# Dynamic convolution and two expert layers on one core: the fold of layer one's tail channels moved off TensorE, and loads and float32 groups replanned

## The chip, the cores and the metric

One core of one Trainium2 chip. The metric is the device time of one execution in microseconds (us), lower is better. The kernel before takes 1397.72 us (median of 3 runs, 1397.65 to 1398.44).

## The reference, cut to what matters

```
attn: w = softmax(weight_gen over K=7 taps); x1[s, d] = sum_k w[s, head(d), k] * x[s - 6 + k, d]
layer 1: h = x1 @ w_in;  g = (a0 + a1 h + a2 h^2 + a3 h^3) / (1 + |b0||h| + |b1| h^2 + 1e-6);  x2 = g @ w_out
layer 2: h = x2 @ w_in2; g = h * clip(h + 3, 0, 6) / 6;                       out = g @ w_out2
```

There are 8192 tokens of 192 channels (2 sequences of 4096), 8 heads, and 2048 hidden channels in both layers. The four weight matrices arrive as 64-bit floats; x and weight_gen are float32.

## The kernel before, in words

**Tiling.** The tokens are cut into 32 units of 256, and a block is one unit. Two units share a chunk: one load of x (`load_chunk`, L105) and one softmax (`softmax_a`, `softmax_e`, `softmax_b`, L132 to L156). A layer's 2048 hidden channels are 16 groups of 128; four groups make a slot of 128x1024 values, so a block has 4 slots and the kernel 128.

**One block.** `conv_mul` and `conv_sum` make the convolution, `xT` transposes it on TensorE into PSUM (L206, L207), `x_hi` and `x_lo` split it into a high and a low float32r part. `in1` multiplies with w_in (five float32r matmuls for each group, `mm_in`, L281) into `h1`, of which there are two buffers in PSUM. A long chain over ScalarE, GpSimd and VectorE (`act_u` to `pool_lo`) makes `ghi` and `glo`, and its step `dve_d` (L370) is the last reader of `h1`. `out1` (L397 to L401) multiplies with w_out and sums a block into one PSUM bank `y1` of two halves: the first 128 output channels, and the tail.

**The fold.** The tail has 64 channels. Its weights `wo1s` hold the high parts in columns 0 to 63 and the low parts in columns 64 to 127, so the tail half of `y1` holds two partial sums, on partitions 0 to 63 and 64 to 127, which must be added. Before, `mid_y` (L229) copies the half to the SBUF tile `ys`, `mid_f` (L250) multiplies it in plain float32 with the constant matrix `fold`, which adds the halves and puts the sum on both, into a bank `yf` of the three-bank ring "s"; `mid_tail` (L257) and `tail_lo` (L264) split `yf` into high and low parts. `mid_head` (L236) and `head_lo` (L243) do so for the first half. `in2` (L281 again), `act_r2`, `dve_g2` and `out2` (L438, plain float32) are layer two; `evac` writes the result.

**Weights.** 28 jobs load 64-bit pieces into a staging ring `st` of 4 buffers (L456), ScalarE and VectorE join the two words to a float32 (`low` L490, `scale` L484, `join` L496, `sign` L503), and `hi` and `lo` split it (L510, L511, L533). The SBUF of the staging ring is reused by layer two's tiles, so `mid_y` of block 0 waits until all jobs are done.

**The order of the work** is not written out: `plan()` places every step on PE, ACT, DVE, POOL or SP by an assumed cost, a priority (a due time from the constants T, CH, XQ, UM ...) and the buffers it takes. Each engine then runs its list in order.

Of the kernel before, what the change touches and what calls it, by code (L numbers as in the profile page):

```python
# [8 lines left out]
F32 = mybir.dt.float32  # L9
# [3 lines left out]
AF = mybir.ActivationFunctionType  # L13
ALU = mybir.AluOpType
# [5 lines left out]
def kernel(  # L20
# [63 lines left out]
        late.append(stage.enter_context(tc.tile_pool(name="late", bufs=2)))  # L84

    ident = const.tile([P, P], F32, name="ident")
    fold = const.tile([P, 2, 64], F32, name="fold")
    acol = const.tile([P, 4], F32, name="acol")
    bcol = const.tile([P, 2], F32, name="bcol")
    bab = const.tile([P, 2], F32, name="bab")  # L90
# [11 lines left out]
    wgt = {}  # L102
    wk = {}

    def load_chunk(c):  # L105
        g = two.tile([P, CT * H, K], F32, tag="wg", name="wg")
        nc.sync.dma_start(
            out=g.rearrange("p (t h) k -> p t (h k)", h=H), in_=wgf[:, c * CT : (c + 1) * CT, :]
        )
        t = two.tile([P, ROWS, D], F32, tag="x", name="x")  # L110
        first = c * CT - (K - 1)
        neg = max(0, -first)
        segs = [(0, P)]
        if neg:
            segs = [(b * S // R + 1, (b + 1) * S // R) for b in range(B)]
            for b in range(B):
                p = b * S // R
                nc.gpsimd.memset(t[p : p + 1, 0:neg, :], 0.0)
                nc.sync.dma_start(
                    out=t[p : p + 1, neg:, :], in_=xf[None, b * S : b * S + ROWS - neg, :]  # L120
                )
        for p0, p1 in segs:
            src = bass.AP(
                tensor=xf.tensor,
                offset=xf.offset + (first + p0 * R) * D,
                ap=[[R * D, p1 - p0], [1, ROWS * D]],
            )
            nc.sync.dma_start(out=t[p0:p1].rearrange("p r d -> p (r d)"), in_=src)
        xch[c] = t
        wgt[c] = g  # L130

    def softmax_a(c):  # L132
        g = wgt[c]
# [92 lines left out]

    def mid_y(b):
        ysb[b] = late[0].tile([P, BMAX], F32, tag="ys", name="ys", bufs=1)[:, : BT[b]]
        nc.scalar.activation(out=ysb[b], in_=y1[b][:, BT[b] :], func=AF.Copy)  # L229

    def mid_head(u):
        b, v = UB[u]
# [13 lines left out]
        )  # L246

    def mid_f(b):
        ps = fold_ps[b] = bank(("mid_f", b), [P, 512], "yf")[:, : BT[b]]
        nc.tensor.matmul(  # L250
            out=ps, lhsT=fold.rearrange("p a d -> p (a d)"), rhs=ysb.pop(b),
            start=True, stop=True,
        )

    def mid_tail(u):
        b, v = UB[u]
# [190 lines left out]
        nc.sync.dma_start(out=of[:, u * 2 : u * 2 + 2, :], in_=o)  # L447

    CW = 512
    ST = 4  # L450

    def load_rows(dst, src):
        srcs = src if isinstance(src, list) else [src]
# [127 lines left out]
                    l(eng)  # L581

    G2 = 11
    T = 9.094
    CH = 5.027
    KP = 0.221
    XP = 17
    LP = 43.011
    LOADP = {(0, "load"): -100.0, (1, "load"): -80.0}
    WIN = 29  # L590
    PEN = 1.976
    CP = 3
    JP0 = 0.189
    JPT = 1.514
    HOLD = 6
    URG = 4.005
    UR = 17.898
    UG = 15.269
    SM = 1.345
    CV = 3.0  # L600
    XTP = 2.0
    XQ = 7.596
    I2 = 2.702
    SPR = 0.483
    O2 = 3.176
    OS = 3.771
    O1 = 1.491
    UM = 1.45
    ops = {}

    def op(key, eng, cost, prio, emit, after=(), take=(), lat=0.15):
# [16 lines left out]
    for n, key in enumerate(order):  # L628
        p = JP0 + n * JPT - (30.0 if n < 2 else 0.0)
        f64, split = WS == 2, key[0] != "o2"  # L630
        sz = 1.0 if key[0] in ("in", "pair") else 0.75
        last = ("job", key, "lo" if split else "sign" if f64 else "load")
        wf = [("wf", 3, [last])] if split else []

        def step(k, eng, cost, prev, take=(), lat=0.15, also=[]):
            op(
                ("job", key, k), eng, cost, LOADP.get((n, k), p - LP * (k == "load")), lambda e=None, key=key, k=k: job_step(key, k, e),
                ([("job", key, prev)] if prev else []) + also, take, lat,
            )

        flex = (("POOL", 1.25 * sz, 0.0), ("DVE", 0.62 * sz, PEN))
        step("load", "SP", 1.46 * sz, None, [("st", ST, [("job", key, "sign")])] if f64 else wf, 2.2)
        if f64:
            step("low", "ACT", 0.55 * sz, "load")
            step("scale", "ACT", 0.55 * sz, "load", [("s", NSB, [("job", key, "sign")])])
            step("join", "DVE", 0.61 * sz, "scale", also=[("job", key, "low")])
            step("sign", "DVE", 0.61 * sz, "join", wf)
        if split:
            step("hi", "ACT", 1.6 if key[0] == "pair" else 0.52 * sz, "sign" if f64 else "load")
            step("lo", flex, 0, "hi")  # L650
        done[key] = last
# [2 lines left out]
    TU = [S0[b] * T - (4 * (BV[b] - 1 - v) + XTP) * T for b, v in UB]  # L654
    for c in range(NCH):
        t = TU[2 * c] - CV * T + 1.9
        add("load", "SP", 3.1, t - XQ * T if c else -90.0, load_chunk, c, lat=2.2, take=[
            ("x", 2, [("conv_mul", 2 * c + 1, 1)]), ("wg", 2, [("softmax_b", c)]),
        ])
        add("softmax_a", "DVE", 0.75, t - SM * T + 2.85, softmax_a, c, after=[("load", c)])  # L660
        add("softmax_e", "ACT", 0.28, t - SM * T + 4.1, softmax_e, c, after=[("softmax_a", c)])
        add("softmax_b", "DVE", 1.5, t - SM * T + T + 6.6, softmax_b, c, after=[("softmax_e", c)],
            take=[("wk", 2, [("conv_mul", 2 * c + 1, 1)])])
    for u, (b, v) in enumerate(UB):
        t = TU[u]
        for i in range(2):
            flex = (("POOL", 2.6, 0.0), ("DVE", 1.6, CP))
            add("conv_mul", flex, 0, t + (2 * i - CV) * T + 1.9, conv_mul, u, i,
                after=[("load", u // 2), ("softmax_b", u // 2)],
                take=[("prod", 1, [("conv_sum", u, i, 1)])])  # L670
# [11 lines left out]
    for b in range(len(BL)):  # L682
        sl = S0[b] + NF // BF[b] - 1
        t = (sl + 2) * T
        add("mid_y", "ACT", 0.2 + BT[b] / 1280, t + 6.05 - UM, mid_y, b,
            after=[("out1", sl, 1), ("late",)], take=[("ys", 1, [("mid_f", b)])])
        add("mid_f", "PE", BT[b] / 590, t + 8.2 - UM, mid_f, b, after=[("mid_y", b)],
            take=[("s", NSB, [("tail_lo", B0[b] + BV[b] - 1)])])
        for v in range(BV[b]):
            u = B0[b] + v  # L690
            add("mid_head", "ACT", 0.4, t + 6.1 + v * 0.1 - UM, mid_head, u, after=[("mid_y", b)],
                take=[("xh1", 2, [("in2", u, NP - 1)])])
            add("head_lo", "DVE", 0.42, t + 7.0 + v * 0.5 - UM, head_lo, u,
                after=[("mid_head", u)] + ([("head_lo", u - 1)] if v else []))
            add("mid_tail", "ACT", 0.4, t + T + 0.65 + v * 0.1 - URG, mid_tail, u,
                after=[("mid_f", b), ("mid_head", u)])
            add("tail_lo", "DVE", 0.42, t + T + 1.35 + v * 0.5 - URG, tail_lo, u,
                after=[("mid_tail", u)] + ([("tail_lo", u - 1)] if v else []))
            tu = t + T + I2 + v * NP * T * SPR
            for q in range(NP):  # L700
# [17 lines left out]
    for sl, (b, q) in enumerate(SL):  # L718
# [3 lines left out]
        for k in range(2):  # L722
# [4 lines left out]
                take=[("h1", 2, [("dve_d", sl)])] if k == 0 else [])  # L727
            add("out1", "PE", 1.18, t + 2 * T + O1 + k, out1, sl, k,
                after=[("pool_lo", sl), done["o1", f1 // 2]] + prev("out1", k),
                take=[("y1", 1, [("head_lo", B0[b] + BV[b] - 1), ("mid_y", b)])] if q + k == 0 else [])  # L730
        add("act_u", "ACT", 1.02, t + 2.25 - CH, act_u, sl, after=[("in1", sl, 1)],
            take=[("u", 1, [("pool_q", sl)])])
        add("act_w", "ACT", 1.25, t + 3.3 - CH, act_w, sl, after=[("act_u", sl), ("bab",)],
# [17 lines left out]
    def coeffs():  # L751
# [4 lines left out]
    op(("bab",), "ACT", 0.2, -1.0,  # L756
       lambda: nc.scalar.activation(out=bab, in_=bcol, func=AF.Abs), [("coeffs",)])

    def plan():
        free = {e: 0.0 for e in ("PE", "ACT", "DVE", "POOL", "SP")}  # L760
        end, rings, users, wait = {}, {}, {}, {}
# [18 lines left out]
        seq = []  # L780
        while len(seq) < len(ops):
            best = None
            for e, rs in ready.items():
# [4 lines left out]
                for o, cost, pen in rs:  # L788
                    at = max([free[e]] + [end[k] for k in o["after"]])
                    for name, depth, _ in o["take"]:  # L790
                        if name == "s":
                            at = max(at, min(open_at(i) for i in range(depth)))
                            continue
                        ring = rings.get(name, [])
                        if len(ring) >= depth:
                            for k in ring[-depth]:
                                at = max(at, end.get(k, float("inf")))
                    rank = (at + pen + KP * max(0.0, o["prio"] - cur - WIN), o["prio"])
                    if at < float("inf") and (pick is None or rank < pick[:2]):
                        pick = (*rank, at, e, cost, o)  # L800
# [2 lines left out]
            _, _, at, e, cost, o = best  # L803
            for f, *c in o["choice"]:
                ready[f].remove((o, *c))
            free[e] = at + cost
            end[o["key"]] = at + cost + o["lat"]
            for name, depth, rel in o["take"]:
# [14 lines left out]
    with tc.manual_schedule():  # L823
        nc.scalar.preload_act_table_set("natural_log_exp_and_others")
        make_identity(nc, ident)
        for e in range(2):
            nc.gpsimd.tensor_tensor(
                out=fold[:, e, :], in0=ident[:, 0:64], in1=ident[:, 64:P], op=ALU.add
            )
        for o, e in plan():  # L830
            o["emit"](*([e] if len(o["choice"]) > 1 else []))

# [29 lines left out]
```

## Time and profile before

| | |
|---|---|
| Median of 3 runs | 1397.72 us |
| The profiled execution, its own time | 1398.85 us |
| Its span (first to last instruction) | 1397.0 us |
| Mean granted TensorE clock | 0.986 |
| Busy share of the span: PE, DVE, ACT, POOL | 93%, 79%, 75%, 79% |
| Chain that ended last, by engine | PE 82%, DVE 6%, ACT 4% |

The profiled execution is 1.13 us above the median, and 1.85 us of it lie outside the span. PE is TensorE, PEld its weight loads, DVE VectorE, ACT ScalarE, POOL GpSimd, and SP the queue that issues every DMA. Matmuls overlap in a trace, so what one takes in a stream is read from one start to the next.

### The profile page before, as it was taken

To read this page: it belongs to the slowest core of one execution; us is meant where nothing else is said; L and a number is where in the kernel's file an instruction comes from. 1 tells how busy PE (TensorE), PEld (TensorE's weight loads), DVE (VectorE), ACT (ScalarE), POOL (GpSimd) and SP (SyncE) were. 2 spreads that over 40 slices of the span, in tenths; PEclk is the share of its full clock that TensorE was granted. 3 is DMA by queue.
4 is the path that set the end of the run, shared out by engine and by line. 5 is a ranking of instruction groups with operands and counts; after the bars stand their busy time and mean duration, and the time that the engine had idled before them with its cause. 6 is when DMAs were issued, how large, how long until landed. Compare 5 with 4: busy or idle time off the path is not lost.

```text
span 1397.0 us, 24025 instructions
## 1 busy us (share of the span) xinstructions
PE 1300.9 (93%) x9920; PEld 1292.0 (92%) x9920; DVE 1109.3 (79%) x1144; ACT 1052.6 (75%) x1326; POOL 1105.4 (79%) x492
## 2 busy tenths in 40 slices
PE   0468999999999999999999999999999999999998
PEld 0458999999999999999999999999999999999998
DVE  4988878788787878878788887878888787887762
ACT  4898777777877777787777778777778877777871
POOL 4898888878788887878878787887878888788670
PEclk9789999999999999999999999999999999999999
DMA  7530010000101000010100001010010100000000
GB/s 186 156 117 30 7 38 6 11 29 7 38 7 38 7 10 29 7 38 7 39 7 7 33 7 38 7 38 7 1 38 7 38 7 7 7 0 7 7 7 12
DMA packets 15765, 37.97 MB, mean 27 GB/s; under 512 B 1832, under 2 KB 12072, under 8 KB 15656
## 3 DMA queue, kind: packets, MB, share of 16 engines
q1 hardware_dynamic: 15656, 36.44, 8.4%
q8 instruction: 78, 1.28, 0.4%
q14 instruction: 31, 0.25, 0.1%
HBM read 30.14 MB, written 6.29 MB: 26 GB/s over the span
## 4 chain that ended last, share of the span: by engine, by line
PE 82%; DVE 6%; ACT 4%; issue 3%; DMA 2%; POOL 2%; SPq 0%; DVEq 0%; POOLq 0%
PE h L281 38%; PE y L438 24%; PE y L400 4%; PE y L401 4%; PE y L398 4%; PE y L399 4%; PE y L397 4%; DVE xc L186 2%; DMA st<-in_moe_w_in_dram 2%; DVE w L370 1%; DVE ghi L358 1%; ACT r L349 1%; ACT r L344 1%; PE yf L250 1%; DMA acol<-in_moe_a_dram 1%
## 5 line engine op out<-in xcount | busy, mean ns | idle before, releaser
L366 POOL TENSOR_TENSOR w<-w,ghi 128x1024 f32<-128x1024 f32 x128 | 308.0, 2406 | 162.4 <-DVE ghi L358 162.3
L438 PE MATMUL y<-wo,g 128*128 128x192 f32 x2048 | 353.4, 326 | 0.0
L329 POOL TENSOR_TENSOR w<-w,u 128x1024 f32<-128x1024 f32 x128 | 308.4, 2410 | 38.8 <-ACT w L315 38.5
L377 POOL TENSOR_TENSOR glo<-w,r 128x1024 fp32r<-128x1024 f32 x128 | 308.0, 2406 | 33.3 <-DVE w L370 18.0
L438 PEld LDWEIGHTS y<-wo,g 128*128 128x128 f32 x2048 | 331.1, 190 | 0.0
L281 PE MATMUL h<-xh,wst 128*128 128x256 f32 x1024 | 292.6, 286 | 0.0
L281 PE MATMUL h<-xl,wst 128*128 128x256 f32 x1024 | 292.3, 285 | 0.1
L358 DVE SCALAR_TENSOR_TENSOR ghi<-h,acol,r 128x1024 fp32r<-128x1024 f32 x128 | 163.7, 1279 | 103.5 <-ACT r L349 103.4
L344 ACT ACTIVATE r<-w 128x1024 f32<-128x1024 f32 x128 | 135.1, 1056 | 117.0 <-POOL w L329 116.7
L419 ACT ACTIVATE r<-h 128x512 f32<-128x512 f32 x256 | 153.3, 599 | 89.3 <-PE h L281 75.8
L333 DVE TENSOR_TENSOR l<-h,l 128x1024 f32<-128x1024 f32 x128 | 156.4, 1222 | 65.3 <-ACT l L322 64.8
L281 PE MATMUL h<-xh,win0hi 128*128 128x256 f32 x512 | 159.1, 311 | 48.5 <-DVE w L370 47.8
L281 PEld LDWEIGHTS h<-xl,wst 128*128 128x128 f32 x1024 | 199.2, 194 | 0.3 <-DVE xl L264 0.3
L281 PEld LDWEIGHTS h<-xh,wst 128*128 128x128 f32 x1024 | 199.0, 194 | 0.1
L424 DVE SCALAR_TENSOR_TENSOR g<-r,h 128x512 f32<-128x512 f32 x256 | 171.6, 680 | 24.6 <-ACT r L419 24.6
L186 DVE TENSOR_REDUCE xc<-prod 128x96 f32<-128x672 f32 x128 | 174.4, 1372 | 20.6 <-POOL prod L171 20.6
L370 DVE SCALAR_TENSOR_TENSOR w<-h,acol,w 128x1024 f32<-128x1024 f32 x128 | 163.7, 1279 | 22.5 <-POOL w L366 20.4
L310 ACT ACTIVATE u<-h 128x1024 f32<-128x1024 f32 x128 | 130.7, 1021 | 53.0 <-PE h L281 52.6
L171 POOL TENSOR_TENSOR prod<-x,wk 128x1344 f32<-128x1344 f32 x64 | 158.1, 2470 | 11.6 <-DVE wk L150 8.0
L337 DVE SCALAR_TENSOR_TENSOR h<-l,acol,h 128x1024 f32<-128x1024 f32 x128 | 164.1, 1282 | 0.1
L315 ACT ACTIVATE w<-u,bab 128x1024 f32<-128x1024 f32 x128 | 159.3, 1244 | 0.0
L397 PE MATMUL y<-ghi,wo1h 128*128 128x256 f32 x512 | 156.1, 305 | 0.0
(71 smaller groups left out, 3256.1 us busy)
## 6 DMA issues: line engine op xcount, KB each, us to landing
x<-in_x_dram SPq DMA_DIRECT2D x14, 960.0 KB, 4.7
st<-in_moe_w_out_dram SPq DMA_DIRECT2D x16, 384.0 KB, 3.6
out_dram<-osb SPq DMA_DIRECT2D x32, 192.0 KB, 1.9
st<-in_moe_w_in_dram SPq DMA_DIRECT2D x8, 512.0 KB, 10.7
st<-in_moe_w_in_dram SPq DMA_DIRECT2D x8, 256.0 KB, 4.7
x<-in_x_dram SPq DMA_DIRECT2D x4, 472.5 KB
wg<-in_weight_gen_dram SPq DMA_DIRECT2D x16, 112.0 KB, 2.7
x<-in_x_dram SPq DMA_DIRECT2D x2, 3.0 KB
```

The lines of the kernel that those rows point to most:

```text
L186: nc.vector.tensor_reduce(out=xc[u][:, i, hs], in_=prod[u, i].rearrange("p k h g -> p (h g) k")[:, hs, :], axis=AX.X, op=ALU.add,)
L281: nc.tensor.matmul(out=dst, lhsT=l[:, fs], rhs=r, start=(n == 0), stop=(n == len(seq) - 1), skip_group_check=True,)
L315: nc.scalar.activation(out=w, in_=e1[sl]["u"], func=AF.Identity, scale=bab[:, 1:2], bias=bab[:, 0:1])
L329: nc.gpsimd.tensor_tensor(out=e["w"], in0=e["w"], in1=e["u"], op=ALU.mult)
L337: nc.vector.scalar_tensor_tensor(out=h, in0=e["l"], scalar=acol[:, 1:2], in1=h, op0=ALU.add, op1=ALU.mult)
L358: nc.vector.scalar_tensor_tensor(out=ghi, in0=h, scalar=acol[:, 0:1], in1=e["r"], op0=ALU.add, op1=ALU.mult)
L366: nc.gpsimd.tensor_tensor(out=m, in0=m, in1=g1[sl][0].bitcast(F32), op=ALU.mult)
L370: nc.vector.scalar_tensor_tensor(out=m, in0=h1.pop(sl), scalar=acol[:, 0:1], in1=m, op0=ALU.add, op1=ALU.subtract)
L377: nc.gpsimd.tensor_tensor(out=glo, in0=e["m"], in1=e["r"], op=ALU.mult)
L397: mm(out=a, lhsT=wo1h[:, n, :], rhs=gh, start=st, stop=False, **kw)
L424: nc.vector.scalar_tensor_tensor(out=fl(g), in0=r, scalar=1.0, in1=fl(h), op0=ALU.min, op1=ALU.mult,)
L438: nc.tensor.matmul(out=y2[u][:, s, :], lhsT=g[:, i, s * P : (s + 1) * P], rhs=wo2[:, n, :], start=(n == 0 and s == 0), stop=(n == NF - 1), ...
```

## The change

The matrix `fold` goes. `mid_y` becomes two ACT copies of 64 partitions each that swap the halves of the tail on the way to `ys`. `mid_f` becomes one DVE addition in place: the tail half of `y1` plus `ys`. `mid_tail` and `tail_lo` read it there, so `y1` is free for the next block only after `tail_lo`; the ring "s" no longer serves the fold. The load of weight_gen is a step of its own (`gen`). The staging ring has 8 buffers. The planner counts loads dearer, puts weight_gen and x of chunk 0 first, and gives weight jobs earlier due times; the convolution of unit 1 waits for the first slot's `in1`; a tie on PE behind an `out2` or `xT` goes to another one of these until 5.5 us of them stand in a row. Nearly all constants of the priorities have new values.

```
-        nc.scalar.activation(out=ysb[b], in_=y1[b][:, BT[b] :], func=AF.Copy)
+        for h in range(2):
+            nc.scalar.activation(
+                out=ysb[b][h * 64 : (h + 1) * 64], in_=y1[b][(1 - h) * 64 : (2 - h) * 64, BT[b] :],
+                func=AF.Copy,
+            )
...
-        ps = fold_ps[b] = bank(("mid_f", b), [P, 512], "yf")[:, : BT[b]]
-        nc.tensor.matmul(
-            out=ps, lhsT=fold.rearrange("p a d -> p (a d)"), rhs=ysb.pop(b),
-            start=True, stop=True,
-        )
+        c = fold_ps[b] = y1[b][:, BT[b] :]
+        nc.vector.tensor_tensor(out=c, in0=c, in1=ysb.pop(b), op=ALU.add)
...
-    ST = 4
+    ST = 8
...
-    T = 9.094
-    CH = 5.027
+    T = 9.201
+    CH = 4.875
...
-    LP = 43.011
-    LOADP = {(0, "load"): -100.0, (1, "load"): -80.0}
-    WIN = 29
+    LP = 60.0
+    J0P = -98.568
+    J1P = -92.851
+    GATED = 2
+    SWL = 5.5
+    LEAD = 4.104
+    X0P = -112.382
+    LOADP = {(0, "load"): J0P, (1, "load"): J1P}
+    WIN = 19.0
...
-    SM = 1.345
+    SM = 1
...
-        step("load", "SP", 1.46 * sz, None, ...
+        step("load", "SP", 2.85 * sz, None, ...
...
-        add("load", "SP", 3.1, t - XQ * T if c else -90.0, load_chunk, c, lat=2.2, take=[
-            ("x", 2, [("conv_mul", 2 * c + 1, 1)]), ("wg", 2, [("softmax_b", c)]),
-        ])
+        add("gen", "SP", 0.6, t - XQ * T if c else X0P, load_gen, c, lat=2.0,
+            take=[("wg", 2, [("softmax_b", c)])])
+        add("load", "SP", 5.3, t - XQ * T + 1.0 if c else X0P + 0.5, load_chunk, c, lat=2.0,
+            take=[("x", 2, [("conv_mul", 2 * c + 1, 1)])])
...
+    def gate(u):
+        b, v = UB[u]
+        sl = S0[b] - 4 * (BV[b] - 1 - v) - int(LEAD)
+        return [("in1", sl, 1)] if 0 <= sl < GATED else []
...
-        add("mid_f", "PE", BT[b] / 590, t + 8.2 - UM, mid_f, b, after=[("mid_y", b)],
-            take=[("s", NSB, [("tail_lo", B0[b] + BV[b] - 1)])])
+        add("mid_f", "DVE", 0.42, t + 6.9 - UM, mid_f, b, after=[("mid_y", b)])
...
-                take=[("y1", 1, [("head_lo", B0[b] + BV[b] - 1), ("mid_y", b)])] if q + k == 0 else [])
+                take=[("y1", 1, [("head_lo", B0[b] + BV[b] - 1), ("tail_lo", B0[b] + BV[b] - 1)])] if q + k == 0 else [])
...
+    FULL = ("out2", "xT")
...
+                    if e == "PE" and 0.0 < run < SWL and o["key"][0] not in FULL:
+                        pen = pen + 0.01
```

## Rows read from the trace of the kernel before

**Rows 1.** The page: busy us of each engine, its share, instructions.

```profile
PE 1300.9 (93%) x9920; PEld 1292.0 (92%) x9920; DVE 1109.3 (79%) x1144; ACT 1052.6 (75%) x1326; POOL 1105.4 (79%) x492
```

**Rows 2.** Windows: stretch, length; busy PE, PEld, DVE, ACT, POOL; clock, DMA share, GB/s.

```profile
0.00:16.00 16.00, 0.00 (x0) 0.00 (x0) 4.68 (x10) 6.02 (x10) 9.14 (x15) 1.00 0.68 181
16.00:32.00 16.00, 0.00 (x0) 0.00 (x0) 8.13 (x10) 7.00 (x13) 6.29 (x4) 1.00 0.85 198
...
96.00:112.00 16.00, 9.41 (x47) 8.34 (x47) 14.17 (x19) 14.09 (x23) 15.77 (x10) 0.71 0.20 58
112.00:128.00 16.00, 16.00 (x133) 16.00 (x133) 12.71 (x14) 13.17 (x17) 12.59 (x6) 0.98 0.18 62
...
622.00:704.00 82.00, 80.35 (x621) 80.00 (x620) 67.69 (x69) 62.97 (x77) 67.21 (x29) 1.00 0.06 19
...
1200.00:1282.00 82.00, 82.00 (x634) 81.90 (x634) 67.01 (x69) 63.47 (x78) 67.59 (x29) 1.00 0.02 6
```

**Rows 3.** All waits: engine, line, waited for: us in total, times, longest.

```profile
PE h L281 <- DVE w L370: 47.8, 19, 15.9
PE xT L206 <- DVE wf L503: 32.3, 1, 32.3
```

**Rows 4.** The chain in order of time, its last piece on PE: start us, us.

```profile
1383.34 10.42 PE y L438 x64
```

**Rows 5.** Timeline of PE in blocks 15 and 16: start us, us, what.

```profile
705.47 0.39 PE L281 MATMUL h<-xh,win0hi 128*128 128x256 f32 x1 [1.56 <-DVE w L370]
...
707.96 2.77 PE L438 MATMUL y<-wo,g 128*128 128x192 f32 x16
...
710.68 0.28 PE L398 MATMUL y<-ghi,wo1l 128*128 128x256 f32 x1
...
723.37 2.77 PE L438 MATMUL y<-wo,g 128*128 128x192 f32 x16
725.97 0.59 PE L250 MATMUL yf<-ys,fold 128*128 128x256 f32 x2
...
726.52 0.28 PE L281 MATMUL h<-xl,win0hi 128*128 128x256 f32 x1
...
729.99 0.28 PE L397 MATMUL y<-ghi,wo1h 128*128 128x256 f32 x1
```

**Rows 6.** Groups by line and form: shapes, count, busy us, mean ns, idle before.

```profile
L229 ACT ACTIVATE ys<-y 128x256 f32<-128x256 f32 x32 | 12.2, 381 | 1.4 <-PE y L401 1.4
...
L533 ACT ACTIVATE wst<-wf 64x512 fp32r<-64x512 f32 x4 | 2.5, 628 | 0.1
L510 ACT ACTIVATE win0hi<-wf 128x512 fp32r<-128x512 f32 x4 | 2.5, 625 | 1.4 <-DVE wf L503 1.4
```

**Rows 7.** Timeline of DVE in the drain of block 15: start us, us.

```profile
727.35 0.41 DVE L264 TENSOR_TENSOR xl<-yf,xh 128x256 fp32r<-128x256 f32 x1
```

**Rows 8.** The start, timelines of SP, POOL, ACT and DVE: start us, us, what.

```profile
9.51 3.02 SPq L128 DMA_DIRECT2D x<-in_x_dram x2
...
19.15 2.46 POOL L171 TENSOR_TENSOR prod<-x,wk 128x1344 f32<-128x1344 f32 x1 [0.55 <-DVE xc L186]
24.67 0.67 ACT L490 ACTIVATE st<-st 128x512 int32<-128x512 uint32 x1 [7.41 <-DMA st<-in_moe_w_in_dram]
...
25.86 0.70 DVE L496 SCALAR_TENSOR_TENSOR dt<-dt,st 128x512 int32<-128x512 int32 x1 [6.86 <-ACT dt L484]
...
30.26 1.33 DVE L186 TENSOR_REDUCE xc<-prod 128x96 f32<-128x672 f32 x1
```

**Rows 9.** Waits of the DMA queue SP.

```profile
SPq L456 <- DVE wf L503: 61.7, 16, 10.2
```

**Rows 10.** DMA issues: count, KB each, median us to landing.

```profile
x<-in_x_dram SPq DMA_DIRECT2D x14, 960.0 KB, 4.7
```

**Rows 11.** Timeline of DVE before PE's wait of 1.56 us: start us, us.

```profile
699.83 2.49 DVE L136 TENSOR_TENSOR wg<-wg,mx 128x224 f32<-128x224 f32 x1
...
704.13 1.28 DVE L370 SCALAR_TENSOR_TENSOR w<-h,acol,w 128x1024 f32<-128x1024 f32 x1
```

More of the change, by code (lines that the diff above doesn't have):

```diff
@@ L86 @@
     ident = const.tile([P, P], F32, name="ident")
-    fold = const.tile([P, 2, 64], F32, name="fold")
     acol = const.tile([P, 4], F32, name="acol")
@@ L103, with load_gen @@
     wk = {}
-    def load_chunk(c):
+    def load_gen(c):
         g = two.tile([P, CT * H, K], F32, tag="wg", name="wg")
@@ L109, in load_chunk @@
         )
+        wgt[c] = g
+    def load_chunk(c):
         t = two.tile([P, ROWS, D], F32, tag="x", name="x")
@@ L129, in load_chunk @@
         xch[c] = t
-        wgt[c] = g
     def softmax_a(c):
@@ L583 @@
     G2 = 11
-    T = 9.094
-    CH = 5.027
-    KP = 0.221
+    T = 9.201
+    CH = 4.875
+    KP = 0.314
     XP = 17
-    LP = 43.011
-    LOADP = {(0, "load"): -100.0, (1, "load"): -80.0}
-    WIN = 29
-    PEN = 1.976
-    CP = 3
-    JP0 = 0.189
-    JPT = 1.514
[L595 to L598, printed above, removed]
-    SM = 1.345
-    CV = 3.0
-    XTP = 2.0
[L602 to L608, printed above, removed]
+    LP = 60.0
[7 more added lines that the diff above has]
+    WIN = 19.0
+    PEN = 2
+    CP = 1.202
+    JP0 = -7.5
+    JPT = 1.514
+    HOLD = 5.0
+    URG = 13.058
+    UR = 13.252
+    UG = 0
+    SM = 1
+    CV = 3.062
+    XTP = 2.0
+    XQ = 6.825
+    I2 = 6.483
+    SPR = 0.445
+    O2 = 8.383
+    OS = 2.686
+    O1 = -1.403
+    UM = 5.922
     ops = {}
@@ L641 @@
         flex = (("POOL", 1.25 * sz, 0.0), ("DVE", 0.62 * sz, PEN))
-        step("load", "SP", 1.46 * sz, None, [("st", ST, [("job", key, "sign")])] if f64 else wf, 2.2)
+        step("load", "SP", 2.85 * sz, None, [("st", ST, [("job", key, "sign")])] if f64 else wf, 2.0)
         if f64:
@@ L656 @@
         t = TU[2 * c] - CV * T + 1.9
-        add("load", "SP", 3.1, t - XQ * T if c else -90.0, load_chunk, c, lat=2.2, take=[
-            ("x", 2, [("conv_mul", 2 * c + 1, 1)]), ("wg", 2, [("softmax_b", c)]),
-        ])
-        add("softmax_a", "DVE", 0.75, t - SM * T + 2.85, softmax_a, c, after=[("load", c)])
+        add("gen", "SP", 0.6, t - XQ * T if c else X0P, load_gen, c, lat=2.0,
+            take=[("wg", 2, [("softmax_b", c)])])
+        add("load", "SP", 5.3, t - XQ * T + 1.0 if c else X0P + 0.5, load_chunk, c, lat=2.0,
+            take=[("x", 2, [("conv_mul", 2 * c + 1, 1)])])
+        add("softmax_a", "DVE", 0.75, t - SM * T + 2.85, softmax_a, c, after=[("gen", c)])
         add("softmax_e", "ACT", 0.28, t - SM * T + 4.1, softmax_e, c, after=[("softmax_a", c)])
@@ L668 @@
             add("conv_mul", flex, 0, t + (2 * i - CV) * T + 1.9, conv_mul, u, i,
-                after=[("load", u // 2), ("softmax_b", u // 2)],
+                after=[("load", u // 2), ("softmax_b", u // 2)] + gate(u),
                 take=[("prod", 1, [("conv_sum", u, i, 1)])])
@@ L684 @@
         t = (sl + 2) * T
-        add("mid_y", "ACT", 0.2 + BT[b] / 1280, t + 6.05 - UM, mid_y, b,
+        add("mid_y", "ACT", 0.3 + BT[b] / 550, t + 6.05 - UM, mid_y, b,
             after=[("out1", sl, 1), ("late",)], take=[("ys", 1, [("mid_f", b)])])
-        add("mid_f", "PE", BT[b] / 590, t + 8.2 - UM, mid_f, b, after=[("mid_y", b)],
-            take=[("s", NSB, [("tail_lo", B0[b] + BV[b] - 1)])])
+        add("mid_f", "DVE", 0.42, t + 6.9 - UM, mid_f, b, after=[("mid_y", b)])
         for v in range(BV[b]):
@@ L694 @@
                 after=[("mid_head", u)] + ([("head_lo", u - 1)] if v else []))
-            add("mid_tail", "ACT", 0.4, t + T + 0.65 + v * 0.1 - URG, mid_tail, u,
+            add("mid_tail", "ACT", 0.4, t + 7.4 + v * 0.1 - URG, mid_tail, u,
                 after=[("mid_f", b), ("mid_head", u)])
-            add("tail_lo", "DVE", 0.42, t + T + 1.35 + v * 0.5 - URG, tail_lo, u,
+            add("tail_lo", "DVE", 0.42, t + 7.9 + v * 0.5 - URG, tail_lo, u,
                 after=[("mid_tail", u)] + ([("tail_lo", u - 1)] if v else []))
@@ L780, in plan @@
         seq = []
+        run = 0.0
         while len(seq) < len(ops):
@@ L805, in plan @@
                 ready[f].remove((o, *c))
+            if e == "PE":
+                run = run + cost if o["key"][0] in FULL else 0.0
             free[e] = at + cost
@@ L825 @@
         make_identity(nc, ident)
[L826 to L829, printed above, removed]
         for o, e in plan():
```

## The prediction

> **What bounds the kernel now.** I read the busy shares first, then windows by stage, then the waits, then PE's own timeline. By the page PE is the only candidate: busy 93% of the span, the others 75 to 79% [rows 1]. An average hides two stages. From 112 us to the end PE runs almost without a gap: 16.00 of 16 us, later 80.35 of 82 and 82.00 of 82, while DVE, ACT and POOL are busy 63 to 68 us of 82 [rows 2]. So in this steady stage a microsecond taken from PE is a microsecond off the time, and the other three have 14 to 19 us free in each pair of blocks. Before 112 us it is the other way round: PE has no matmul until 32.3 us [rows 3], and from 96 to 112 us only 47 while POOL is busy 15.77 of 16 us [rows 2]. PE's clock there is low too (0.71), but that follows from its waits.
>
> What is left over in the steady stage is one wait in two blocks: PE waits for `dve_d` (L370) to free a buffer of `h1`, 19 times, 47.8 us together, the longest 15.9 us in the start [rows 3]. The usual one is 1.56 us [rows 5], and the window of two blocks shows 82 - 80.35 = 1.65 us idle [rows 2]. About 15 pairs of blocks make some 25 us.
>
> **The profiled execution** is the base: 1398.85 us, span 1397.0, with 1.85 us around it; the median of the runs is 1.13 us lower, and I subtract that at the end. A difference under 0.2%, 2.8 us, is no change here.
>
> **The fold leaves PE.** From the start of the `out2` group at 723.37 us to the second matmul behind the fold at 726.52 us are 3.15 us [rows 5]. The group itself is 16 x 0.163 = 2.60 us, since 64 such matmuls take 10.42 us [rows 4], and one float32r matmul is 16 / 133 = 0.12 us [rows 2]. The fold's two passes are what remains: 3.15 - 2.60 - 0.12 = 0.43 us. There are 32; the first falls in the start, where PE waits anyway, so 31 x 0.43 = **-13.3 us**, all on the engine that sets the end.
>
> **What takes its place.** A second ACT copy per block: one of 128 partitions takes 381 ns, and half the partitions cost the same, since 64x512 from the upper half to the lower takes 628 ns and 128x512 takes 625 [rows 6]. So ACT gets 32 x 0.38 = 12 us. DVE gets an addition of 128x256 with one operand in PSUM; `tail_lo` is such an instruction and takes 0.41 us [rows 7]: 32 x 0.41 = 13 us. Both lie beside PE: DVE goes from 67.7 to 68.5 us of 82, ACT from 63.0 to 63.8 [rows 2]. I count 0. Without that cover they cost at most 0.79 x 32 = 25 us.
>
> **`y1` is held longer.** The first `out1` of the next block must now wait for `tail_lo`, not `head_lo` and `mid_y`. In block 15 `tail_lo` ended at 727.35 + 0.41 = 727.76 us, and the first `out1` of block 16 started at 729.99 [rows 5, 7]: 2.2 us of slack under the new rule. The drain gains a copy and an addition (0.79 us) and loses the fold with its place behind 2.60 us of `out2` [rows 5], so I count 0.
> The rule that speaks against it is in the Trainium skill, Perfetto Trace Analysis, section Matmuls: independent matmul groups should rotate through PSUM banks, so that the evacuation of one overlaps the next group's matmuls. By the rule this edit gives a stall in each block, by the row none until the drain is 2.2 us late; the rule's outcome is the last rival below.
>
> **Float32 groups.** If a switch between float32 and float32r cost PE something, longer runs would save it. From 707.96 to 710.68 us, across the group and the switch back, are 2.72 us; 16 x 0.163 + 0.12 is 2.72 [rows 4, 5]. The switch costs nothing that shows, so grouping gains 0. It can lose: in a run `in1` and `in2` stand behind up to 10.42 us of `out2` [rows 4], and ACT and DVE have less to do. I take 0, the nearest row being the switch itself; a loss would show as longer waits on `h1`.
>
> **The start.** DVE sat idle for 6.86 us before 25.86 us, for a weight job whose bytes ACT awaited for 7.41 us; behind it in DVE's list stood a `conv_sum` (30.26 us) whose input POOL had ready at 19.15 + 2.46 = 21.6 us [rows 8]. PE's first transpose came after that. Ahead of the late weights SP had issued x of chunk 1 at 9.51 us [rows 8], needed only for block 2. Such a chunk is 960 KB and lands in 4.7 us [rows 10]; at the 198 GB/s of the window [rows 2] it is 4.8 us, with 112 KB of weight_gen 5.4. The change puts jobs ahead of chunk 1, and counts a load at 2.85 instead of 1.46 us, so that the planner no longer puts waiting work in front of ready work. The 8 staging buffers bear on SP's waits for the ring, 61.7 us in 16 waits [rows 9]. Moving x and weight_gen of chunk 0 to the front delays the first weight job by about 5 us and hastens the first product; these are the same DMAs. The gate on unit 1 takes 2.46 us products and their sums out of the way.
> What is it worth at 112 us, where the steady stage begins? Upper bound: the start can be shortened by what its fullest engine idles. POOL is idle for 16 - 9.14 = 6.9 us of the first 16 and 16 - 6.29 = 9.7 us of the next 16 [rows 2], DVE and ACT for more; later they are nearly full, and no staging buffer makes them faster. That is 16.6 us. Lower bound: 0, if POOL, busy 15.77 of 16 us, sets the end whatever arrives first; a loss of 5 us if the later first weight job counts. I take **-8 us**, near the 5.4 us of the chunk and below the 6.86 + 5.4 that would add up only if nothing else bound.
>
> **The wait of the steady stage.** The 1.56 us wait comes from the subtraction of `softmax_a`, 2.49 us at 699.83 us, in front of the `dve_d` at 704.13 us [rows 11], which the plan counts with 0.75 us for the whole step. That count stays; but SM goes from 1.345 to 1 with T about 9.2, which makes the step due some 3 us later, and all other priorities change too. Bounds: -25 us (the waits go) and +25 us (one in each block). I take **-5 us**: the nearest rows show both a pair with the wait and one without [rows 2], and the new order has less PE work to hide it.
>
> **Sum:** -13.3 - 8 - 5 = -26.3 from 1398.85, so 1372.5, and by 1.13 less against the median: **1371 us**.
>
> **Rivals.**
> - *The waits go altogether and the start gains in full*: 1397.7 - 13.3 - 16.6 - 25 = 1343 us; with one of the two at half, about 1355. For it: DVE has 14 us free in 82. Against: `dve_d` stays in a list where a mis-costed step can precede it.
> - *Only the fold counts*: loads come earlier, but POOL and ACT set the end of the start and the waits stay: 1397.7 - 13.3 = 1384 us. For it: POOL's 15.77 of 16 us. This is also the case where the replanned loads do not do what they are meant to.
> - *Slower: the drain of `y1`.* One place: the first `out1` of each block, behind mid_y, the addition, `mid_tail` and `tail_lo`. If two of these stand behind a long instruction of 1.28 us each and one behind the 2.49 us subtraction [rows 11], `tail_lo` is later by 0.79 + 2.56 + 2.49 = 5.8 us, less the 2.60 us of `out2` that it no longer waits for: 3.2 us, which is 1.0 us beyond the slack of 2.2. It decides from 0.85 us beyond, which in 31 blocks undoes the 26.3; at 1.0 us the time is 1397.7 - 26.3 + 31 = 1402 us. Against it: 2.2 us of slack and a drain that loses the fold's wait.
>
> **Chances.** The forecast 0.50, waits gone 0.20, only the fold 0.17, the drain 0.09, and 0.04 that gains and losses cancel within 2.8 us. So faster 0.87, same 0.04, slower 0.09. The range goes from 1350, between forecast and first rival, to 1390, which takes in the fold alone with a start slower by 5 us.
>
> **What would show it.** Right: no L250 on PE; two copies of about 0.38 us at L230 or so on ACT and an addition near 0.42 us on DVE for each block; PE still at 80 of 82 us, but two blocks in about 81 us; PE's first transpose well before 32 us and its dense stage before 112; the wait for L370 no longer than 1.7 us. Wrong: the gap before the first `out1` of a block waiting for `tail_lo`; waits for L370 in each block or of several us; a start that ends at 112 us with the loads landed earlier; PE's float32 runs followed by idle time.

## The result, and the profile after

| | before | after |
|---|---|---|
| Median | 1398.08 us (runs beside it) | 1362.2 us (4 runs, 1360.96 to 1362.31) |
| Ratio to before | | 0.974 [0.9723, 0.9757] |
| The profiled execution, and its span | 1398.85 us, 1397.0 us | 1362.24 us, 1360.3 us |
| Two blocks in the steady stage | 81.87 us | 79.23 us |

The change makes the kernel 35.9 us faster. The forecast was 1371 us, with a range of 1350 to 1390. The direction and the range hold. The sum holds less well than it looks: one term was five times too small, one is nearly nothing, one loss was not in it at all, and one edit that was costed at nothing cannot be taken out again without losing the whole gain.

The page of the kernel after, busy us of each engine, its share and its instructions; it answers to [rows 1]:

```profile
PE 1288.7 (95%) x9856; PEld 1283.8 (94%) x9856; DVE 1090.3 (80%) x1176; ACT 1053.5 (77%) x1358; POOL 1099.7 (81%) x490
```

PE has 64 instructions fewer, ACT and DVE 32 more each. The windows of the kernel after, columns as in [rows 2]:

```profile
0.00:16.00 16.00, 0.00 (x0) 0.00 (x0) 2.74 (x7) 2.24 (x4) 5.21 (x9) 1.00 0.83 168
16.00:32.00 16.00, 7.27 (x30) 6.31 (x31) 11.96 (x16) 11.03 (x21) 11.30 (x7) 1.00 0.94 257
...
96.00:112.00 16.00, 13.46 (x74) 12.69 (x73) 11.75 (x13) 12.63 (x17) 13.55 (x7) 0.68 0.00 1
...
622.00:704.00 82.00, 82.00 (x638) 81.93 (x637) 68.88 (x76) 65.68 (x84) 68.33 (x30) 1.00 0.06 19
```

In the steady window PE is busy for all 82 us, where before it was 80.35, and does 638 matmuls in place of 621. In the first 16 us DVE, ACT and POOL are less busy than before (2.74, 2.24 and 5.21 us against 4.68, 6.02 and 9.14), in the next 16 more (11.96, 11.03 and 11.30 against 8.13, 7.00 and 6.29), so that over the 32 us they have done a little more. PE's last wait of the start ends at 106.38 us, where it was 110.26, and from 96 to 112 us PE is busy 13.46 of 16 us, where it was 9.41. What PE waits for in the kernel after, answering to [rows 3] (us in total, times, longest):

```profile
PE xT L207 <- DVE wf L505: 19.4, 1, 19.4
PE h L283 <- DVE w L372: 17.7, 4, 13.7
...
PE y L402 <- POOL glo L379: 7.0, 3, 4.6
...
PE h L283 <- DVE g L426: 3.0, 1, 3.0
```

Of the 19 waits for `dve_d` (L372 now) 4 are left, three of them in the start and one of 1.25 us near the end. Between 112 and 1270 us PE waits for nothing, while before it waited 14 times there, 21.9 us in all or 1.56 each (some of the expectations below have 1.66). The chain of waits of the kernel after (start us, us, what), first its piece at the start, then one row of the steady stage that comes again two blocks later:

```profile
2.14 10.70 DMA x<-in_x_dram
...
628.04 8.40 PE h L283 x70
...
707.27 8.40 PE h L283 x70
```

Two blocks take 707.27 - 628.04 = 79.23 us. Before, a row of the chain that comes again two blocks later was

```profile
651.88 7.20 PE h L281 x60
...
733.75 7.20 PE h L281 x60
```

so two blocks took 81.87 us. I use this period below, since it is a finer measure than a busy share or a wait: a wait of 1.56 us will turn out to be worth 1.82 us of the period.

### The profile page after: what moved, and what is told of

The parts are those of the page before. It is cut to its first block, busy times and chain, and to the rows that moved or that the text cites. A ratio compares the mean times of both kernels' runs of the same rounds, so it can differ in the third digit from the quotient of the medians.

```text
span 1360.3 us, 23977 instructions
## 1 busy us (share of the span) xinstructions
PE 1288.7 (95%) x9856; PEld 1283.8 (94%) x9856; DVE 1090.3 (80%) x1176; ACT 1053.5 (77%) x1358; POOL 1099.7 (81%) x490
## 3 DMA queue, kind: packets, MB, share of 16 engines
HBM read 30.14 MB, written 6.29 MB: 27 GB/s over the span
## 4 chain that ended last, share of the span: by engine, by line
PE 91%; ACT 4%; POOL 2%; DVE 1%; issue 1%; DMA 1%; SPq 0%; POOLq 0%; DVEq 0%; ACTq 0%
PE h L283 44%; PE y L440 24%; PE y L402 4%; PE y L400 4%; PE y L401 4%; PE y L399 4%; PE y L403 4%; DMA x<-in_x_dram 1%; POOL prod L172 1%; POOL w L368 1%; PE xT L208 0%; PE xT L207 0%; ACT st L492 0%; ACT dt L486 0%; DVE w L372 0%
## 5 line engine op out<-in xcount | busy, mean ns | idle before, releaser
L440 PE MATMUL y<-wo,g 128*128 128x192 f32 x2048 | 348.3, 326 | 0.0
L372 DVE SCALAR_TENSOR_TENSOR w<-h,acol,w 128x1024 f32<-128x1024 f32 x128 | 163.5, 1277 | 43.6 <-POOL w L368 43.6
L312 ACT ACTIVATE u<-h 128x1024 f32<-128x1024 f32 x128 | 130.4, 1019 | 64.5 <-PE h L283 64.4
L421 ACT ACTIVATE r<-h 128x512 f32<-128x512 f32 x256 | 146.6, 595 | 41.9 <-PE h L283 24.1
L324 ACT ACTIVATE l<-h,acol 128x1024 f32<-128x1024 f32 x128 | 154.1, 1204 | 0.0
## 6 DMA issues: line engine op xcount, KB each, us to landing
x<-in_x_dram SPq DMA_DIRECT2D x4, 472.5 KB
```

Of the source, the lines that this page charges most:

```text
L372: nc.vector.scalar_tensor_tensor(out=m, in0=h1.pop(sl), scalar=acol[:, 0:1], in1=m, op0=ALU.add, op1=ALU.subtract)
L440: nc.tensor.matmul(out=y2[u][:, s, :], lhsT=g[:, i, s * P : (s + 1) * P], rhs=wo2[:, n, :], start=(n == 0 and s == 0), stop=(n == NF - 1), ...
```

## The experiments

Each kernel was timed beside the kernel before on the same chip; all ratios are to the kernel before (1397.93 to 1400.43 us in these runs). A difference to the kernel after is one of medians from different chips, on which the kernel before itself differs by up to 2.5 us; where that matters, the ratios decide.

### The fold alone

The kernel before with the two copies and the addition; the order of every list stays.

```diff
+        for h in range(2):
+            nc.scalar.activation(out=ysb[b][h * 64 : (h + 1) * 64], in_=y1[b][(1 - h) * 64 : (2 - h) * 64, BT[b] :], func=AF.Copy)
...
+        c = fold_ps[b] = y1[b][:, BT[b] :]
+        nc.vector.tensor_tensor(out=c, in0=c, in1=ysb.pop(b), op=ALU.add)
```

> The kernel before with the fold alone changed: two copies that swap the halves and an addition on DVE, in the old order of every engine, loads and priorities untouched; the result is the same. Theory A (the fold's 0.43 us of PE per block is saved whole in any order): 1398.1 - 13.3 = 1385 us, 1383 to 1388, and the wait of 1.66 us for dve_d in each second block stays. Theory B (the old order gives the saved time back as longer waits for dve_d, since the addition and the copy load DVE and ACT): 1392 to 1398 us with waits of 2 us and more.

1393.59 us, ratio 0.9966 [0.9955, 0.9977]: 4.6 us faster, a third of what the fold costs on PE. PE's timeline, one period apart, and PE's waits:

```profile
701.79 0.39 PE L282 MATMUL h<-xh,win0hi 128*128 128x256 f32 x1 [1.55 <-DVE w L371]
...
783.14 0.39 PE L282 MATMUL h<-xh,win0hi 128*128 128x256 f32 x1 [1.55 <-DVE w L371]
```

```profile
PE h L282 <- DVE w L371: 46.5, 19, 15.2
```

The period is 783.14 - 701.79 = 81.35 us, 0.52 less than before, though 2 x 0.43 us of matmuls left PE. The long wait for `dve_d` is where it was. The chain of waits between 620 and 800 us says why:

```profile
722.83 0.35 DVE y L254
...
740.39 1.29 DVE w L371
741.73 2.65 PE h L282 x20
```

From the new addition (L254) it runs over ACT, POOL and DVE to the `dve_d` of the other block of the pair, and PE goes on 0.06 us behind the end of it (741.67, 741.73). Before, PE came to this place 0.37 us after its `dve_d` had ended (745.22, 745.59). From the long wait to this place are now 39.94 us, 0.18 less than before, and from there to the next long wait 41.41, 0.33 less, which makes the 0.52. So in the old order the loop from `h1` over these engines back to `dve_d` is in both blocks nearly as long as PE's own work, and PE, made shorter by 0.43 us in each, waits for it. The rest of the loss is at the end: PE waits 1.3, 0.5 and 0.2 us for steps of the drain there.

### The fold put back into the kernel after

```diff
-        for h in range(2):
...
+        nc.scalar.activation(out=ysb[b], in_=y1[b][:, BT[b] :], func=AF.Copy)
...
+        nc.tensor.matmul(out=ps, lhsT=fold.rearrange("p a d -> p (a d)"), rhs=ysb.pop(b), start=True, stop=True)
```

> The kernel after with the fold put back on PE as a float32 matmul into its own bank, one copy and no addition, in the new order of every engine; the result is the same. Theory A: 1362.2 + 13.3 = 1375.5 us, 1373 to 1378. Theory B (in the new order the fold would lie beside waits or lengthen the drain of y1): 1362 to 1368 if hidden, over 1380 if the wait for the bank costs more than the 0.43 us.

1376.4 us, ratio 0.9842 [0.9827, 0.9858], 14.2 us above the kernel after. The chain of waits and the steady window:

```profile
632.20 8.40 PE h L283 x70
...
712.29 8.40 PE h L283 x70
```

```profile
622.00:704.00 82.00, 82.00 (x634) 81.88 (x633) 67.80 (x72) 63.11 (x81) 68.24 (x29) 1.00 0.06 19
```

The period is 80.09, 0.86 above 79.23, which is 0.43 us for each fold. So the price of the prediction is right to the hundredth, and it is paid in full where the order leaves no waits. The missing waits do not come from the fold: between 112 and 1270 us they are gone here too, with the fold still on PE.

### The kernel before without the subtraction

The wait was put down to the 2.49 us subtraction of `softmax_a`. This kernel leaves the subtraction of the maximum out.

```diff
-        nc.vector.tensor_tensor(
-            out=g, in0=g, in1=mx[:, :, None].to_broadcast([P, CT * H, K]), op=ALU.subtract
-        )
```

> The kernel before without the subtraction of the maximum in softmax_a (the softmax is then taken of the unshifted values), order untouched. It takes the 2.49 us instruction from DVE in front of dve_d. Theory A (PE's wait of 1.66 us in each second block is that instruction's length): the waits vanish, 1398.1 - 25 = 1373 us, 1370 to 1377. Theory B (POOL's pool_m or the chain behind it sets dve_d): waits stay over 1 us and the time is 1388 to 1398 us.

1373.54 us, ratio 0.982 [0.9803, 0.9837]: 24.6 us faster. PE's waits, and the chain one period apart:

```profile
PE h L278 <- DVE w L367: 25.3, 4, 15.9
```

```profile
637.82 7.20 PE h L278 x60
...
717.87 7.20 PE h L278 x60
```

The period is 80.05 us, 1.82 less than before, so the wait of 1.56 us is gone and a little more, and the period is that of the kernel after with its fold put back (80.09). One subtraction in two blocks, 16 in all and 2.49 us long in the steady stage, cost 24.6 us.

### Both of these in the kernel before

```diff
+        c = fold_ps[b] = y1[b][:, BT[b] :]
+        nc.vector.tensor_tensor(out=c, in0=c, in1=ysb.pop(b), op=ALU.add)
...
-            out=g, in0=g, in1=mx[:, :, None].to_broadcast([P, CT * H, K]), op=ALU.subtract
```

> Both: the kernel before with the new fold and without the subtraction of the maximum, old order and old loads. Theory A (the whole gain is the fold and these waits, and the replanned loads add nothing net): 1398.1 - 13.3 - 25 = 1360 us, 1357 to 1364. Theory B (the two overlap, or the loads carry a part of the gain): 1368 us and more.

1368.42 us, ratio 0.9787 [0.9771, 0.9804]: 29.7 us faster, where the parts from the two ends (24.6 + 14.2) would give 39. The chain, one period apart:

```profile
675.19 7.20 PE h L279 x60
...
754.72 7.20 PE h L279 x60
```

The period is 79.53 us, 0.30 above the kernel after, and the end waits for the drain as in the fold alone. So the old order loses a part of the fold even without the subtraction.

### The due time of the softmax

Two kernels: the kernel before with SM = 1, and the kernel after with SM = 1.345.

```diff
-    SM = 1.345
+    SM = 1
```

> The kernel before with SM = 1 instead of 1.345, one constant: in the steady stage it moves softmax_a behind other steps in DVE's list (PE's list changes in 8 rows, POOL's and SP's in none). Theory A (PE's wait in each second block is made by where the subtraction stands, in front of dve_d and beside a POOL instruction): the waits of 1.66 us vanish or nearly, 1371 to 1379 us, and the subtraction's mean falls below 2 us. Theory B (the place does not matter, some other new constant removes the waits): 1393 to 1398 us.

> The kernel after with SM = 1.345, the old value, all else as after. Theory A: the subtraction is back in front of dve_d, waits of 1 to 1.7 us in each second block come back, 1362.2 + 15 to 25 = 1377 to 1387 us. Theory B (the new order is robust without it): 1360 to 1366 us.

The first takes 1383.27 us, ratio 0.9877 [0.9857, 0.9897]; the second 1362.93 us, ratio 0.973 [0.9711, 0.9749], as the kernel after. The subtraction by line and form (count, busy us, mean ns), in the first and in the second, and the second's steady window:

```profile
L136 DVE TENSOR_TENSOR wg<-wg,mx 128x224 f32<-128x224 f32 x16 | 35.2, 2198 | 0.6
```

```profile
L137 DVE TENSOR_TENSOR wg<-wg,mx 128x224 f32<-128x224 f32 x16 | 36.7, 2293 | 0.6
```

```profile
622.00:704.00 82.00, 82.00 (x637) 81.97 (x636) 70.03 (x76) 65.70 (x83) 68.54 (x30) 1.00 0.06 19
```

The subtraction is as slow as before in both (2198 and 2293 ns). In the kernel before its later place halves the wait; its waits between 112 and 1270 us fall from 21.9 to 9.7 us. In the kernel after it can be slow and costs nothing, and that although a `dve_d` stands close behind it. This is the second kernel:

```profile
685.11 2.63 DVE L137 TENSOR_TENSOR wg<-wg,mx 128x224 f32<-128x224 f32 x1
...
688.79 1.27 DVE L372 SCALAR_TENSOR_TENSOR w<-h,acol,w 128x1024 f32<-128x1024 f32 x1
```

```profile
691.42 0.41 PE L283 MATMUL h<-xh,win0hi 128*128 128x256 f32 x1
```

`dve_d` starts 1.05 us behind the end of the subtraction, nearer than the 1.81 us of the kernel before [rows 11]. But PE comes for the buffer that it frees only at 691.42 us, 1.36 us after its end; before, PE stood waiting and went on 0.06 us after it (705.41, 705.47) [rows 5, 11]. So neither the constant, nor a shorter subtraction, nor its distance from `dve_d` removes the waits by itself: in the new order PE has other work until the late `dve_d` is done. Which of the other constants gives it that slack was not separated.

### The float32 groups undone

```diff
-    SWL = 5.5
+    SWL = 0.0
```

> The kernel after without the grouping of float32 steps on PE (SWL = 0), so out2 and xT are mixed with float32r steps as the other priorities have it. Theory A (a switch costs nothing): 1360 to 1366 us, differences only by waits in the last blocks. Theory B (the groups save something at each switch): 1368 us and more, with the same PE waits.

1423.65 us, ratio 1.0167 [1.0148, 1.0187]: some 60 us slower than the kernel after. Its steady window, its waits and its products on DVE:

```profile
622.00:704.00 82.00, 79.34 (x605) 77.97 (x604) 69.85 (x71) 61.82 (x78) 64.13 (x27) 1.00 0.06 19
```

```profile
PE h L283 <- DVE w L372: 27.1, 18, 13.8
...
PE h L283 <- DVE g L426: 19.4, 29, 3.0
PE y L402 <- POOL glo L379: 18.0, 32, 4.7
```

```profile
L172 DVE TENSOR_TENSOR prod<-x,wk 128x1344 f32<-128x1344 f32 x14 | 52.1, 3719 | 0.0
```

The time of the kernel rises by 4.36 us in each two blocks by the same repeated row of the chain (664.80 and 748.39 us, 83.59): PE waits four to five times in them, for three different things, and does 605 matmuls in the window in place of 638. The kernel after has POOL do all 64 convolution products; here 14 moved to DVE, and they take 3.72 us each there. The next kernel forbids DVE these products; PE's and ACT's lists are the same as in this one.

```diff
-            flex = (("POOL", 2.6, 0.0), ("DVE", 1.6, CP))
+            flex = (("POOL", 2.6, 0.0), ("DVE", 1.6, 1e6))
```

> The kernel after with SWL = 0 as in the third run before, and the product of the convolution never on DVE: there 14 of 64 products went to DVE, where one takes 3.72 us against 1.6 us in the planner's count. The lists of PE and ACT are those of that run, row for row. Theory A (the 61 us were these products, in front of dve_d and dve_g2): 1362 to 1372 us. Theory B (the order of out2 on PE itself makes the waits): 1400 us and more.

1421.46 us, ratio 1.0163 [1.0146, 1.018]. So the products are not the cause; the new lists are. SWL is a rule for PE, but the plan answers to it on every engine: the lists of ACT, DVE and POOL differ from those of the kernel after as well, and no run separates them from PE's. On PE one difference stands out: of the four `out2` groups of a block the kernel before runs each by itself (16 matmuls), the kernel after two by themselves and two as a double of 32, the kernel with SWL = 0 all four in doubles. So in the steady stage the rule that was to group float32 steps leaves fewer of them together than its absence does. Whether that makes the waits stays open, since no run here varied it alone.

### The loads

The kernel after with the loads planned as before (ten constants), and with 4 staging buffers alone.

```diff
-    ST = 8
+    ST = 4
-    LP = 60.0
-    J0P = -98.568
-    J1P = -92.851
-    GATED = 2
-    X0P = -112.382
+    LP = 43.011
+    J0P = -100.0
+    J1P = -80.0
+    GATED = 0
+    X0P = -90.0
...
```

> The kernel after with the load plan of before: 4 staging buffers, the old assumed costs of loads, the old due times of jobs and chunks, no gate. Theory A (the start only shifts: PE begins 13 us earlier but idles 12 us more before 106 us, so the loads are worth 1 to 2 us): 1361 to 1366 us, with PE's first transpose at 30 us or later. Theory B (the loads carry 5 us or more of the gain): 1367 to 1375 us.

> The kernel after with 4 staging buffers instead of 8, all other constants as after; PE's list is unchanged. Theory A (the buffers let SP issue weights earlier, and that carries the 10 us that the old load plan costs): 1368 to 1374 us. Theory B (order and assumed cost of the loads carry them, or the buffers only shorten waits of SP that nobody waits for): 1360 to 1365 us.

1372.37 us, ratio 0.9802 [0.9779, 0.9824], 10.2 us above the kernel after by the medians and 8.7 by the ratios; with 4 buffers alone 1364.69 us, ratio 0.9756 [0.9739, 0.9772], 2.5 us above it and within 0.2%. Two windows of the kernel with the old loads, and PE's first instruction in it:

```profile
16.00:112.00 96.00, 43.03 (x229) 40.92 (x230) 78.21 (x100) 79.08 (x130) 77.73 (x53) 0.75 0.45 134
112.00:220.00 108.00, 103.30 (x804) 101.93 (x804) 91.89 (x91) 81.91 (x104) 84.88 (x36) 1.00 0.07 24
```

```profile
17.60 0.45 PE L207 MATMUL xT<-ident,xc 128*128 128x128 f32 x1 [17.60 <-DVE xc L187]
```

and the same windows of the kernel after:

```profile
16.00:112.00 96.00, 47.78 (x246) 44.66 (x247) 80.29 (x103) 85.03 (x142) 82.99 (x57) 0.75 0.48 139
112.00:220.00 108.00, 108.00 (x846) 107.87 (x845) 92.64 (x96) 85.52 (x105) 91.33 (x39) 1.00 0.07 24
```

PE begins even earlier than in the kernel after (17.60 against 19.4 us) and yet has less done: 4.75 us less busy by 112 us, and another 4.70 us less in the next 108. The output of block 3 is copied out 8.35 us later (at 277.17 against 268.82 us), and this lag stays until the last blocks, which add 1.2, so nearly all of the loss is one of the start. An early first matmul is no measure of a start. SP's waits for the staging ring are 37.5 us in 14 waits in the kernel after, 61.7 in 16 before [rows 9].

### What sets the start: ScalarE, or the first x

First the kernel after without its 28 `low` instructions on ScalarE; then the kernel after with the x loads of chunks 0 and 1 cut otherwise.

```diff
-        nc.scalar.activation(
-            out=low, in_=low.bitcast(U32), func=AF.Copy, scale=0.936 * 2.0 ** -29
-        )
```

> The kernel after without the 28 ACT instructions that convert the low words of the weights (some 16 us of ACT before 106 us); the join takes the high word in their place, so the weights are other numbers. All lists else as after. Theory A (ACT, busy 15.9 and 16.0 of 16 us in 32 to 64 us, sets the pace of the start): the dense stage of PE begins 5 us or more earlier, 1350 to 1357 us. Theory B (POOL, DVE or the landing of the loads set it): 1359 to 1364 us.

1360.75 us, ratio 0.9726 [0.9708, 0.9744]. ACT's work in the first 112 us falls from 87.27 to 74.65 us by the windows, and the time by 1.4 us, within 0.2%; the output of block 1 is copied out 0.1 us earlier (189.48 against 189.59). So ScalarE's work does not set the pace of the start.

```diff
-            segs = [(b * S // R + 1, (b + 1) * S // R) for b in range(B)]
+            segs = [(b * S // R + i, b * S // R + j) for b in range(B) for i, j in ((1, 16), (16, 64))]
```

> The kernel after, but x of chunks 0 and 1 is loaded in pieces of 15 and 48 partitions instead of 63; nothing else is changed, and the order of every other instruction stays. In the kernel after the two 63-partition loads of chunk 0 (472.5 KB each) stand on the chain of the start for 10.7 us, while a whole chunk of 128 partitions (960 KB) lands in 4.7 us, and the Trainium skill (DMA: Bandwidth & Descriptors, section Why a DMA increments its semaphore by 16 and not by 1) has an uneven partition count feed fewer engines: 63 gives 9, 48 gives 16 and 15 gives 15. Theory A (the first product waits for these bytes, and an earlier one carries through to the steady stage): the first POOL product starts 4 to 5 us earlier than at 13.0 us, PE's first transpose starts before 16 us instead of at 19.4, and the time is 1357 to 1360 us. Theory B (the start is set by POOL, DVE and ACT and by the order of their lists, and the weight jobs arrive as before): the product and the transpose come earlier, but the idle time moves to PE's next waits, and the time is 1361 to 1364 us.

1360.91 us (5 runs, 1358.76 to 1361.18), ratio 0.9727 [0.9714, 0.9741]. The chain of waits of this kernel, from the first load into the steady stage:

```profile
3.09 7.15 DMA x<-in_x_dram
10.40 2.47 POOL prod L172
...
92.10 4.14 PE h L283 x20
...
626.58 8.40 PE h L283 x70
```

In the kernel after the same three pieces behind the load (2.14 us, 10.70 long) begin at 13.00, 95.18 and 628.04 us. So the first product comes 2.6 us earlier (4 to 5 were expected), the chain is 3.1 us ahead at 92 us and 1.46 us ahead in the steady stage. The theory that the first x is on the path is right in kind; half of what it gives is lost again before the steady stage, so the time lies between the two ranges. 1.3 us under the kernel after is below what these runs can tell from no change, and the two intervals overlap; it beats the kernel before clearly.

## Why the prediction was right, and where it was not

**The fold, -13.3: right, in the new order only.** Put back, it costs 14.2 us, and the period shows the 0.43 us per fold that the rows of before gave. "All on the engine that sets the end" was wrong for the kernel before, where it gave 4.6. The step that failed is the reading of [rows 2]: 14 to 19 us free in 82 on the other engines is a mean, and a loop over all of them can still be nearly as long as PE's work, as it was in the fold alone.

**What takes its place, 0: right.** The copies and the addition in the kernel after, by line and form:

```profile
L231 ACT ACTIVATE ys<-y 64x256 f32<-64x256 f32 x64 | 24.2, 378 | 10.9 <-PE y L403 9.8
...
L255 DVE TENSOR_TENSOR y<-y,ys 128x256 f32<-128x256 f32 x32 | 13.5, 423 | 7.2 <-ACT xh L241 7.2
```

378 ns for half the partitions and 423 ns for the addition are the values taken (381 and 0.41). In the old order they are not free: the addition lies on the loop there.

**`y1` held longer, 0: right, so the slowest rival fell.** The drain and the next `out1` in the kernel after:

```profile
698.97 0.42 DVE L255 TENSOR_TENSOR y<-y,ys 128x256 f32<-128x256 f32 x1
...
700.96 0.42 DVE L266 TENSOR_TENSOR xl<-y,xh 128x256 fp32r<-128x256 f32 x1
...
703.43 0.36 PE L399 MATMUL y<-ghi,wo1h 128*128 128x256 f32 x1
```

`tail_lo` (L266) ends at 701.38 us and `out1` starts at 703.43, 2.05 us later; in the other block of the pair at 741.00 and 744.32, 3.3 us. The rule of the Trainium skill that spoke against the edit (Perfetto Trace Analysis, section Matmuls) gave no stall here (PE waits for nothing between 112 and 1270 us): one bank is drained in place while PE has other work for it.

**The wait of the steady stage, -5: mis-sized.** It was 24.6 us by the run without the subtraction, the far end of its bounds. The step that failed is "the nearest rows show both a pair with the wait and one without, and the new order has less PE work to hide it". The mechanism named for the wait, a long subtraction ahead of `dve_d`, was right for the kernel before, and the rival "waits gone altogether" had this half right. The reason given for its going, the new SM, was not: alone it halved the waits in the old order and changed nothing in the new one, and there is slack for `dve_d` where the prediction saw less PE work to hide it.

**The start, -8: about 1.** The parts that the runs give are -14.2 and -24.6, together -38.8; the result is -35.9, so the start and the end together lose 2.9 us. The traces of the two kernels between which this lies, the kernel before without the subtraction and the kernel after with the fold put back, tell the one from the other, since their periods are alike (80.05 and 80.09 us). In both the output of block 1 is copied out when the steady stage has begun:

```profile
189.94 0.49 ACT L443 ACTIVATE osb<-y 128x384 f32<-128x384 f32 x1 [1.15 <-PE y L435]
```

```profile
189.06 0.47 ACT L448 ACTIVATE osb<-y 128x384 f32<-128x384 f32 x1
```

So the start gains 0.9 us. From the same copy of block 27, at 1230.63 and 1230.18 us, to the end of the span are 139.6 and 142.3 us, so the end loses 2.6, a term that the prediction did not have. (From the kernel before itself to the kernel after the copy of block 1 moves by 3.5 us, from 193.13 to 189.59, but in that the first of the 1.56 us waits and the first folds are counted already.) In the kernel after PE waits 1.3 and 3.0 us in the last 90 us, in the kernel before 0.5 in the last 122.

```profile
1276.35 0.39 PE L283 MATMUL h<-xh,win0hi 128*128 128x256 f32 x1 [1.25 <-DVE w L372]
...
1318.77 0.58 PE L283 MATMUL h<-xh,win1hi 128*128 128x256 f32 x1 [2.98 <-DVE g L426]
```

PE's first matmul came 12.9 us earlier (19.4 against 32.3), as foretold, and the time went into the next waits. The failing step is "so the start can be shortened by what its fullest engine idles": by the chain the start runs over x, POOL, ACT and DVE in turn, and the fullest engine is only a part of it. The replanned loads still matter: without them the new order would lose 8.7 us by the ratios.

**Float32 groups, 0: wrong, the largest miss.** By [rows 4, 5] the switch between float32 and float32r costs nothing; no run tests that by itself. But "grouping gains 0" does not follow from it: the constant changes the lists of all engines, and without it the other constants give 1423.65 us, slower than the kernel before. The prediction named only a loss by grouping, and its step "I take 0, the nearest row being the switch itself" priced the switch where the order was at stake. PE's waits for `dve_d`, `dve_g2` and `pool_lo` (64.5 us in that kernel, 27.7 in the kernel after) are more than half of the difference. That the new order would have lost its gain without this edit could not be read from the trace of before.

So the sum came within 9 us because a term that was 20 us too small stood against a start that was 7 too large and an end that was left out. That is in part luck.

## What to carry to other kernels

Where a planner makes the lists, an edit's price on the bounding engine (0.43 us for a fold) is what it gives only if the order leaves no waits; the same edit gave 4.6 us in one order and 14.2 in another. Size a steady wait by its period, and take its cause away alone to see what it is worth, before counting what moves beside it. A late step costs only what exceeds the slack until the next engine comes for its result. A start is read along its chain, not from the time of the first matmul.

## What the runs showed of the hardware

**A subtraction that takes 0.39, 1.40 or 2.49 us.** The same 128x224 instruction took 0.39 us in the start. One of the kernel before, with what POOL did at that time:

```profile
699.65 2.42 POOL L366 TENSOR_TENSOR w<-w,ghi 128x1024 f32<-128x1024 f32 x1 [2.21 <-DVE ghi L358]
```

and one of the kernel after, with POOL beside it:

```profile
690.09 2.43 POOL L379 TENSOR_TENSOR glo<-w,r 128x1024 fp32r<-128x1024 f32 x1
...
691.37 1.40 DVE L137 TENSOR_TENSOR wg<-wg,mx 128x224 f32<-128x224 f32 x1
```

Before, it starts at 699.83 us [rows 11], 0.18 us behind POOL's product, and ends at 702.32, 0.25 us behind that product's end at 702.07. After, it starts 1.28 us into POOL's instruction and ends at 692.77, again 0.25 us behind POOL's end at 692.52. In the kernel after with SM = 1.345 the subtraction of 2.63 us ends at 687.74, 0.26 us behind the end of POOL's product at 687.48. It looks as if it does its work only when POOL is done. The Trainium skill has a rule that fits: in SBUF — State Buffer, section Who interferes with whom, a DVE instruction with two inputs in SBUF contends with a GpSimd instruction that reads SBUF, and the order of issue decides which of the two is blocked. These rows agree; no run here put the two side by side by themselves. In these rows the length of the step is set by where it falls against POOL, so that a planner's fixed 0.75 us for the step cannot be right in every place.

**A load of 63 partitions was slow.** On the chain the first x takes 10.70 us in two loads of 63 partitions, 472.5 KB each, where a chunk of 960 KB over 128 partitions lands in 4.7 us [rows 10]. In pieces of 15 and 48 it took 7.15. The Trainium skill (DMA: Bandwidth & Descriptors, section Why a DMA increments its semaphore by 16 and not by 1) has the number of engines that serve a load be the largest divisor, at most 16, of its outer size, so 9 for 63, but 16 for 48 and 15 for 15. The times agree in direction; the traces here do not show how many engines served a load. Why 7.15 us is still above 4.7 stays open; weight loads run beside it.
